# A retention layer and an MLP-mixer block in one kernel: the order of its work planned anew with another model of the transfers

## The chip, the core and the metric

The kernel runs on one core of a Trainium2 chip. The core has a tensor engine (PE, with its weight loads shown apart as PEld), a vector engine (DVE), a scalar engine (ACT), GpSimd (POOL) and a sync engine (SP). Each engine takes its instructions in the order in which the program holds them, and an instruction that has to wait holds up all that stand behind it on its engine. SP, ACT and POOL also issue DMA transfers.

The metric is the device time of one execution, in microseconds (us). Before the change it was 192.45 us in the median of three runs, 190.45 us the lowest and 193.12 us the highest.

## What is computed

```python
# attention part: a decayed running state for each head (4 batches, 8 heads, 768 steps, 64 wide)
for t in range(S):
    state = gamma * state + einsum('bhd,bhe->bhde', k[:, :, t], v[:, :, t])
    y[:, :, t] = scale * einsum('bhd,bhde->bhe', q[:, :, t], state)
x = y with the heads side by side             # 4 x 768 x 512
# mixer part
h = maximum(xT @ w_tok1, 0) @ w_tok2          # over the 768 steps, 256 wide inside
u = x + hT
out = u + maximum(u @ w_ch1, 0) @ w_ch2       # over the 512 channels, 1536 wide inside
```

## The kernel before, in words

**Tiles and stages.** A batch has 768 steps, held as 6 chunks of 128. Its 8 heads are taken in 4 pairs. `front(b, p)` does the attention part and the token mixing for one pair, `back(b)` the channel mixing of a whole batch.

A front works like this. The loads bring k, q and v (lines 464 and 467, issued by POOL). k and q are multiplied by powers of the decay on ACT, DVE or POOL ("decays", lines 506 and 508). k and q are then turned so that channels lie on partitions: for batch 0 and 1 on PE (lines 530 and 532), for batches 2 and 3 by DMA transposes that SP issues (line 520, tiles kT and qT). PE forms the chunk states (561), and DVE runs the decay over them (571, 573). PE forms the scores (599), DVE masks them (609, tile am), and PE sums them with v (621) and with the state (633). Then follow the two products of the token mixing (656 and 676) and the evacuations to x, u and X (line 643). The front ends with turning u into uT, for some pairs on PE (715) and for most by a DMA transpose from SP (705).

A back has a wide part and a narrow part. In batches 0 and 1 the wide part is plain products (749) with a ReLU on ACT (765). In batches 2 and 3 `widen7` forms it from seven products in place of eight (818), for which DVE first takes four differences of uT (line 788, tile hs), ACT keeps partial sums (829) and DVE adds (838). The narrow part is `narrow7` (967 and 977), with sums of h on DVE (931), partial sums kept by ACT (957) and additions to X on DVE (984); its rows go out by DMA (1008), from SP or ACT. The last rows of batch 3 use a plain form (893, 902, 908).

**Modes of PE.** Products with 64 rows or 64 columns (530, 561, 599, 633) run with PE in another shape of its array than the others. The planner's code calls them "high" and "wide" (`tiled`).

**What sets the order.** The kernel first makes a list of 1217 operations (`Op`) with dependencies, buffers and a cost for each engine that may do them. `PRECEDENCE` gives each a rank: it holds two base-36 digits for each operation, in the order of rank. `arrange` then walks through time with a model of five engines, of eight PSUM banks and of the transfers (`Rings`). Whenever an engine is free it takes the operation of lowest rank that the model says is ready. The order in which the operations were taken is the order in which instructions are written, and so the order on each engine; it also decides between ACT and DVE where both can do an operation. The model has no part in the run itself.

`Rings` holds the transfers. The fields of a transfer are a number of steps and the time of one step: `dma=(48, 24)` for a DMA transpose. The queues of SP, POOL and ACT share the transfer engines in rounds, with `MIX` added to a round for each further queue. When the last step is done, the transfer lands `LAND` later, and `PAD` after that once 25 us are past. A transpose that is issued while POOL's queue holds a transfer lands `WAIT` = 4,000 ns later still.

POOL's loads stand in an order written out by hand (`ORDER`), and each must follow the one before it (`behind`). In the first 21 us the program puts PE products of zeros (line 1085) where the plan has PE idle.

Eight of the transfers from SP and ACT can be under way at a time: in the trace they use eight semaphores (101 and 112 to 118) in turn, so the ninth waits for the landing of the first. POOL's loads have eight of their own (103 to 110).

## Time and profile before

| | us |
|---|---|
| median of three runs (lowest, highest) | 192.45 (190.45, 193.12) |
| the profiled execution's own time | 191.84 |
| its span, from the first instruction to the last | 190.1 |
| PE busy | 180.0 (95%), 2347 matmuls |
| DVE busy | 148.3 (78%) |
| ACT busy | 131.2 (69%) |
| POOL busy | 53.0 (28%) |
| PE doing products of zeros (line 1085) | 9.4, 35 matmuls |

The granted clock of PE was 1.00 in all stretches. POOL's queue moved 13.18 MB and its packets took 86.7% of the span of sixteen transfer engines; the queue of SP and ACT moved 10.69 MB and took 35.1%. A DMA transpose of uT landed 7.8 us after its issue in the median (3.0 to 12.0), one of kT or qT 8.5 us (2.7 to 11.0), a load of q 9.4 us (4.6 to 17.0).

A busy PE is not PE at its peak: ends of matmuls are modelled, so that a short stop between two products can be inside "busy". The chain of work that ended last gives the time from one start to the next, and there such stops are seen.

### The profile page before, as it was taken

How to read it: one execution, taken by the hardware profiler on the slowest of the kernel's cores; microseconds unless marked ns; L12 is line 12 of the kernel's file. 1: busy time of each engine (PE TensorE's matmuls, PEld its weight loads, DVE VectorE, ACT ScalarE, POOL GpSimd, SP SyncE). 2: the span in 40 equal slices, each digit the busy share in tenths (PEclk: the TensorE clock that was granted, in tenths of full speed). 3: DMA queues.
4: the chain of work that ended last, by engine and by line, in shares of the span. 5: the costliest groups of instructions: out<-in, count | busy, mean ns of one | idle time of the engine just before them, and what ended most of it. 6: DMA issues, size and time to landing. Idle time of an engine off the chain costs nothing.

```text
span 190.1 us, 5757 instructions
## 1 busy us (share of the span) xinstructions
PE 180.0 (95%) x2347; PEld 134.5 (71%) x2347; DVE 148.3 (78%) x401; ACT 131.2 (69%) x306; POOL 53.0 (28%) x62
## 2 busy tenths in 40 slices
PE   7987797999999999999999999799999999999993
PEld 3544686666678889667778889556578996656882
DVE  4698885823999996945199799498999959997982
ACT  6367599599689956689987956679864363665120
POOL 8995676550395013055002820000000000000000
PEclk9999999999999999999999999999999999999999
DMA  6999999999999999999999999992200168000116
GB/s 106 170 156 195 184 177 182 182 205 203 167 157 155 111 157 186 118 198 191 134 134 136 157 171 150 202 237 45 43 3 0 59 124 240 2 0 0 59 57 221
DMA packets 94236, 25.54 MB, mean 134 GB/s; under 512 B 84353, under 2 KB 91265, under 8 KB 94209
## 3 DMA queue, kind: packets, MB, share of 16 engines
q0 software_dynamic: 67456, 13.18, 86.7%
q1 hardware_dynamic: 26032, 10.69, 35.1%
q10 hardware_dynamic: 720, 1.31, 2.4%
q8 instruction: 18, 0.29, 0.7%
q14 instruction: 10, 0.07, 0.1%
HBM read 26.74 MB, written 6.29 MB: 174 GB/s over the span
## 4 chain that ended last, share of the span: by engine, by line
PE 78%; DMA 10%; POOL 4%; DVE 3%; issue 1%; ACT 1%; DVEq 0%; POOLq 0%; ACTq 0%
PE bank L749 17%; PE bank L818 13%; PE bank L967 13%; PE bank L977 10%; DMA uT<-u 6%; PE bank L676 6%; PE bank L656 5%; DMA v<-in_v_dram 5%; PE bank L893 3%; PE bank L599 3%; PE bank L621 2%; PE bank L561 2%; POOL k L467 2%; PE bank L633 2%; PE bank L530 1%
## 5 line engine op out<-in xcount | busy, mean ns | idle before, releaser
L609 DVE TENSOR_TENSOR am<-bank,mask 128x384 f16<-128x384 f32 x64 | 31.6, 547 | 8.0 <-PE bank L599 7.7
L749 PE MATMUL bank<-uT,wc 128*128 128x384 f16 x192 | 36.2, 327 | 0.0
L467 POOL DMA_DIRECT2D v<-in_v_dram x16 | 16.5, 1032 | 48.7 <-PE bank L621 43.8
L765 ACT ACTIVATE h<-bank 128x384 f16<-128x384 f32 x48 | 22.8, 513 | 4.7 <-PE bank L749 4.3
L749 PEld LDWEIGHTS <-wc 128*128 128x128 f16 x192 | 16.9, 98 | 9.8 <-DVE U L573 0.5
L829 ACT COPY us<-bank 128x384 f32<-128x384 f32 x36 | 16.7, 490 | 8.6 <-PE bank L818 5.4
L957 ACT COPY us<-bank 128x256 f32<-128x256 f32 x33 | 12.2, 380 | 15.0 <-PE bank L967 13.0
L984 DVE TENSOR_TENSOR X<-X,bank 128x256 f32<-128x256 f32 x44 | 17.8, 413 | 4.2 <-PE bank L977 3.7
L838 DVE TENSOR_TENSOR h<-bank,us 128x384 f16<-128x384 f32 x36 | 18.7, 550 | 2.6 <-ACT us L829 1.6
L967 PEld LDWEIGHTS <-hs 128*128 128x128 f16 x198 | 18.5, 98 | 2.5
L573 DVE SCALAR_TENSOR_TENSOR U<-U,gp,bank 128x64 f32<-128x64 f32 x64 | 17.0, 277 | 1.3
L643 ACT CAST u<-bank 128x384 f16<-128x384 f32 x31 | 14.9, 496 | 4.2 <-PE bank L676 4.1
L967 PE MATMUL bank<-wsum,hs 128*128 128x256 f16 x132 | 17.7, 273 | 0.0
L643 ACT CAST x<-bank 128x384 f16<-128x384 f32 x31 | 14.0, 484 | 5.1 <-PE bank L621 3.8
L467 POOL DMA_DIRECT2D k<-in_k_dram x15 | 15.5, 1034 | 3.3 <-DVE U L573 1.1
L506 ACT ACTIVATE k<-k,gk 128x384 f16<-128x384 f16 x21 | 12.7, 619 | 4.6 <-DMA k<-in_k_dram 3.6
L643 ACT COPY X<-bank 128x384 f32<-128x384 f32 x32 | 15.6, 503 | 0.0
L676 PE MATMUL bank<-h,wt 128*128 128x64 f16 x384 | 15.3, 193 | 0.0
L676 PEld LDWEIGHTS <-wt 128*128 128x128 f16 x384 | 14.1, 98 | 1.6
L818 PE MATMUL bank<-hs,late 128*128 128x384 f16 x72 | 14.5, 326 | 0.3 <-ACT us L829 0.2
L931 DVE TENSOR_TENSOR hs<-h 128x768 f16<-128x768 f16 x18 | 9.8, 550 | 5.3 <-ACT h L765 5.3
L977 PEld LDWEIGHTS <-h 128*128 128x128 f16 x132 | 12.5, 98 | 1.9
(84 smaller groups left out, 342.7 us busy)
## 6 DMA issues: line engine op xcount, KB each, us to landing
...
q<-in_q_dram POOLq DMA_DIRECT2D x16, 192.0 KB, 9.4
v<-in_v_dram POOLq DMA_DIRECT2D x16, 192.0 KB, 9.2
k<-in_k_dram POOLq DMA_DIRECT2D x15, 192.0 KB, 10.6
...
```

Source lines behind the costliest of these rows:

```text
L467: (nc.sync if hard else nc.gpsimd).dma_start(out=tile_of(s, [P, 2, NC, D], FP if hard else F16), in_=src.rearrange("h (c p) d -> p (h c) d ...
L573: nc.vector.scalar_tensor_tensor(out=u[:, c], in0=u[:, c - 1], scalar=gp[:, p:p + 1], in1=st, op0=ALU.mult, op1=ALU.add)
L609: nc.vector.tensor_tensor(am, SC[g].tile[:, :m * P].rearrange("p (i t) -> p i t", t=P), mask.to_broadcast([P, m, P]), ALU.mult)
L643: (nc.scalar.copy if e == "ACT" else nc.vector.tensor_copy)(tile(), cols(src.tile[:, :S // 2]))
L676: nc.tensor.matmul(Y[j].tile[:, i * D:(i + 1) * D], wt2[:, jt, t], H1.tile[:, jt, j * D:(j + 1) * D], start=False, stop=(jt == NJ - 1), sk ...
L749: nc.tensor.matmul(acc[:, :SH], wc1[:, ct, ft * P:(ft + 1) * P], UT.tile[:, ct, sh * SH:(sh + 1) * SH], start=(ct == 0), stop=(ct == NP - 1))
L765: nc.scalar.activation(H2.tile[:, ft], A.tile[:, :SH], AF.Relu)
L818: nc.tensor.matmul(acc[:, :SH], left(ct), r[:, ct], start=first and ct == 0, stop=ct == C2 - 1, skip_group_check=True)
L838: nc.vector.tensor_tensor(h(m, sh), R.tile[:, :SH], KS.tile[:, j], ALU.add)
L967: nc.tensor.matmul(acc_[:, lo], l[:, j], r[:, j], start=first and j == 0, stop=j == K2 - 1, skip_group_check=True)
L977: nc.tensor.matmul(acc_[:, lo], l[:, j], r[:, j], start=first and j == 0, stop=j == K2 - 1, skip_group_check=True)
L984: (nc.vector if e == "DVE" else nc.gpsimd).tensor_tensor(dst(), dst(), b_(), ALU.add)
```

## The change

The model of the transfers is altered, a rule for the eight semaphores comes in, and `PRECEDENCE` is another list of the same 1217 operations. `MIX` and `SLOW` (which was 1.0) go. In place of `MIX`, POOL's queue takes `PULL` = 2.2 shares of a round whenever another queue is active. `WAIT` now holds for all transfers from SP and ACT after 25 us, stores too, and not for transposes from SP alone. A transpose has steps of 16.6 ns in the model and not 24. `lane` has a transfer from SP or ACT wait, in the model, for the landing of the eighth before it. `arrange` makes the new order from the new ranks by this model. No operation, tile, buffer, hand-written order or cost of PE, ACT or DVE is altered, and neither is what an operation emits. [...]

```diff
--- before.py
+++ after.py
@@ -44,9 +44,8 @@
     FIRST = dict(SP=600, POOL=1300, ACT=700)
     LAND = dict(SP=900, POOL=1900, ACT=2000)
     DT = 40.0
-    MIX = 8.0
+    PULL = 2.2
     WAIT = 4000
-    SLOW = 1.0
     PAD = 300
 
     def __init__(self):
@@ -59,7 +58,7 @@
         end = first + op.dma[0] * self.GEN[q]
         self.made[q].append(end)
 
-        late = self.WAIT if q == "SP" and op.dma[0] == 48 and self.line["POOL"] else 0
+        late = self.WAIT if q != "POOL" and start > 25000 and self.line["POOL"] else 0
         self.line[q].append([op, float(op.dma[0]), first, end, late])
 
     def busy(self):
@@ -69,11 +68,10 @@
         dt, t = self.DT, self.t
         on = [(q, l[0]) for q, l in self.line.items() if l and l[0][2] <= t]
         if on:
-            round_ = sum(x[0].dma[1] for _, x in on) + self.MIX * (len(on) - 1)
-            if t > 25000:
-                round_ *= self.SLOW
+            share = {q: self.PULL if q == "POOL" and len(on) > 1 else 1.0 for q, _ in on}
+            round_ = sum(share[q] * x[0].dma[1] for q, x in on)
             for q, x in on:
-                n = dt / round_
+                n = share[q] * dt / round_
                 if x[3] > t:
                     n = min(n, dt / self.GEN[q])
                 x[1] -= n
@@ -101,7 +99,7 @@
     free = dict(FREE)
     taken = {t: [] for t in BUFS}
     bank_slot = {i: None for i in range(8)}
-    sp_made = [0, 0, 0]
+    lanes = []
     waiting = {e: [] for e in ENGINES}
     for o in ops:
         for w in o.ways:
@@ -172,6 +170,12 @@
                     m = max(m, x)
         return m, banks
 
+    def lane(o, e):
+        if o.dma is None or e == "POOL" or len(lanes) < 8:
+            return 0
+        x = end[lanes[-8].n]
+        return INF if x is None else x + SEM
+
     left = n
     while left:
         moved = False
@@ -190,6 +194,7 @@
                         wake = min(wake, r)
                     continue
                 m, banks = room(o)
+                m = max(m, lane(o, e))
                 if m > t:
                     if m < INF:
                         wake = min(wake, m)
@@ -211,6 +216,8 @@
                 free[e] = at + way[1]
                 if o.dma:
                     rings.add(e, o, t)
+                    if e != "POOL":
+                        lanes.append(o)
                     if e == "SP":
                         free[e] = max(t + way[1], rings.made["SP"][-3])
                 else:
@@ -256,29 +263,29 @@
 
 
 PRECEDENCE = (
-    "0c312g322j2i0b0k380a07342535420h432n0i27300j28000403080105020e0d2209230g0f2444332h2k3e3d260l3y293i2l2m3z3f2a"
...
-    "c6c7atbeavkhktkibfauc8ljbga31mbhawc9bil4caa4cba7bja61nl5cca8a5cd9mjk999nai9c9o9d9pjnlvaacel6a9laajlkaxlbcfkj"
...
-    "b6cid3m5mncjn5d5dvd4chm6d6modwd7n6bqd8dxclmp1ocnd9e1dabtmqdbe2mse4mre5e6cmdydzbumte31pcomue0lme7ln1qbvmacpmb"
-    "mxlobw1rmcbzcqbxmzmyc01smvn0byncc2n1crn3c1mw1tcvnlcsn2n4dcctnmn8cwddcunrcycxnon9nansegnnnpnbdfdenqdgnendntdh"
-    "n7nunfngdinvdje8njdknhe9dleanyecfndmebnznwnifonkdno3euevfpnxdoo7o0dpo4ewo9eddqefereseeo1obo6o8osetocodo2ouog"
...
-    "orp7p4fup3p8p9fvopekpqelpsfxp6prpefyq7emptpvpfpgpufzphpwpbpienpcpyeopopjpzpxeqpdepplpppkq0q5f4qof8pmq6q2q1f5"
...
+    "0a070900050b04010c0302080d060e340f35420g43220h262327240i2530310j322f0k332g2h282j3d290l3g3e3y3i3z2a3f400m4w4x"
...
+    "a2kld1atlba3bdlcl8bea4bfl9kybga5bhkzbikma6knl0aubja71mkobkava8bmldaw1nleaabla9kvaxbokwlfbpbnbrd2aykxbqd3d51o"
+    "dvdwc9d4d6l1d7azl2cabsd8lgcbl3d9b0dxccbtdalhcdb1kscektdbm7b2m8cfb3dydzlmbukue0b4lnmdlimjmfbvb5b6ljmem9bzmklo"
...
+    "e6dhcse7mldi1tm5ctlvculwm6mmlxdje8mnfnfocvecdkmqfpebcwmae9eumbeamrnpcydlmumcmvernlmxedesdmmwnmnqmyeefqnrnnet"
+    "cxnoefevnunsdno7ewfrn5ntego8donvn6fsehexo9ftdpdreydqfueiezdsfvf0fwnydtduf1fxejf2nwfynzoaf3f4nxfzo3f8f5eko0f7"
+    "elf6enemmzn3eoo1f9epn0eqfan4fbg0n1fcn8o4fdg1o6nag4n9g2fenbncn2ffg3nendn7fgo2nhfhnfo5fjfingobfkodninjocosfmoz"
...
 )
@@ -519,7 +526,7 @@
                     t = tile_of(dst, [P, S], F16)
                     nc.sync.dma_start_transpose(out=t.rearrange("d (c t) -> d c t", t=P),
                                                 in_=src.tile.rearrange("p c h d -> p (c h d)"))
-                return Op(ops, (PLACE[b, p], 0, b, p, 0), [("SP", 1200, 1200, emit)], dep, [dst], [src], dma=(48, 24))
+                return Op(ops, (PLACE[b, p], 0, b, p, 0), [("SP", 1200, 1200, emit)], dep, [dst], [src], dma=(48, 16.6))
             T = Slot(FA)
 
             def emit():
@@ -705,7 +712,7 @@
                 nc.sync.dma_start_transpose(out=UT.tile[:, p].rearrange("d (c t) -> d c t", t=P),
                                             in_=U16.tile.rearrange(flat))
             e = Op(ops, (PLACE[b, p], 0, b, p, 99), [("SP", 1200, 1200, emit)], casts + [None if opens else first_of[b, "uT"]],
-                   [UT] if opens else [], [U16] if opens else [U16, UT], dma=(48, 24))
+                   [UT] if opens else [], [U16] if opens else [U16, UT], dma=(48, 16.6))
         else:
             T = Slot(FA)
 
```

More of the change, by code (lines that the diff above doesn't have):

```diff
@@ L258 @@
 PRECEDENCE = (
-    "0c312g322j2i0b0k380a07342535420h432n0i27300j28000403080105020e0d2209230g0f2444332h2k3e3d260l3y293i2l2m3z3f2a"
-    "400m4w4x3g414y2b3h0n2e4z362c3j2d3k37390o3a4b3b2o3c2f4e2p3l453m4d3n0p462q4748492r4a0q504c514g0r4f2s595b2t4h5c"
-    "4i0s2w2v3o524j3p532u0t2x544k3q552y565a4l0u3t2z5d3r4m3s575e585f0v5u5y5v3u5h5g4n5z3w3v4o0w5i6u3x5j4r4p6v5k0x4q"
-    "4s6q5w0z6r4u4t5x5m0y4v5p06675ngs6a5o6s5q69gj5r6b5s6t686w605t6xgm116y616c6zgt62hm7063hn7164gn72hs65ht66gk6dgl"
-    "127q6egu7rh76fgoh8hj136ghkhdh9hehl7n6h7m14hogp6igqhf7sgr7o7thu6j7u7pi77v157wgv7xh46kh17yh26lhph3hqi8hr10ha16"
@@ L264 @@
-    "i95lhb6mhc736nh5746o6phyh676gwhz7517gx7z77gy8178hv8279gz80hg83h0hhhwi0181uhi84i1hxi21w8520i37a8o867bjb1v87ig"
-    "7c19ijih8iia1xiiib7d8j1ajc88ili4icik7e1bi58pim8mi68q7i8n1c8k9f7f9g89jx8r1y8l1didie8s7ginif1eiu7h8t1zio8b8uis"
-    "1f7jjr9iip217l8a7k8eitjt8civ9jiwjs8d9kiqiy8f1gjuixjv8gjyizae8hj1irjwafj08v9hagj2j3j98wj48zk0ab8xack28yk1ad90"
-    "jz92jalsj5k4k3lg91ldj6lek6k51hjej8k7k9jfjdk895kakb96kc1ib7jib8jgjjb9jp9397jh9a989l9bak9e9qjl9sal9rjoj79v94jq"
-    "9u9wlhlfamltjmanm1m29tlikdlukem3kmkfl1l29zah9xl3ao9yaskvc31jkwaqkga0l7arl8l9kx1kbdksapc4a1knc5babb1lkoa2kubc"
@@ L269 @@
-    "c6c7atbeavkhktkibfauc8ljbga31mbhawc9bil4caa4cba7bja61nl5cca8a5cd9mjk999nai9c9o9d9pjnlvaacel6a9laajlkaxlbcfkj"
-    "llkkaylcczd0kykzklckkpd1azkql0lykrb3bklzb0mdm0mhb1mfb2memimgb4m7bmbsb5lwm8bnlxlpm9lqmjblbolrm4mkbpbrmlcgd2mm"
-    "b6cid3m5mncjn5d5dvd4chm6d6modwd7n6bqd8dxclmp1ocnd9e1dabtmqdbe2mse4mre5e6cmdydzbumte31pcomue0lme7ln1qbvmacpmb"
-    "mxlobw1rmcbzcqbxmzmyc01smvn0byncc2n1crn3c1mw1tcvnlcsn2n4dcctnmn8cwddcunrcycxnon9nansegnnnpnbdfdenqdgnendntdh"
-    "n7nunfngdinvdje8njdknhe9dleanyecfndmebnznwnifonkdno3euevfpnxdoo7o0dpo4ewo9eddqefereseeo1obo6o8osetocodo2ouog"
@@ L274 @@
-    "oaeho5drqbqmfcqzqhr0qnrvq4fdr1otoeexohofoxovdsozoyeyojduowdtezf0fqp0okf1frolp1oqfsfwpap5f2ejomonoip2f3eiftoo"
-    "orp7p4fup3p8p9fvopekpqelpsfxp6prpefyq7emptpvpfpgpufzphpwpbpienpcpyeopopjpzpxeqpdepplpppkq0q5f4qof8pmq6q2q1f5"
-    "qqqppnf6q3qrqtf7q8qvf9quqcqefaqdqwqsgdqxqfshq9rrqas0r3rwqgrsfeqyr4rtqjsjffqiskr2sds2s1qkrusifgses4qlfhslsmsg"
-    "fis5s3fbg7g0sfsns6g3g4s9g2sog1rxs7sag5s8g6spr9sbg8ryg9r5t4fjsqrzfkr6tkscragaflr7fmsrrer8gbtnrgrfgcrhgfrbggss"
-    "gercgighrdristrksurjsxrlrmrnsvrpt3rosyu1szrqtdt0uit5t1tlt8t2tpt9tmt6tat7tbtstouptttrtitutztjtftetvu0twtgvnvi"
@@ L279 @@
-    "txujswu3thu2tyunu4u6u8tquouku5u7uzuluqu9urx5uauxugubusumuyuuutuhuducuvvgv1uev0x6uwvhufxqxlv2v4vlvjv5v3vmvkxm"
-    "v6v7vov8w1tcvpv9vevqvvvfvbvavrvwvsvcwnvtx7wjx8vuwowkx9xawlwsvdxbwuwmwtxcw3vxwvw2wpvzvywyw4w6w0wqw8w7w5wrwww9"
-    "wzwawxwcx0wbxnx3wdwewgwhxexdx1wiwfxfx4xhx2xixgxoxjxkxrxsxp"
+    "0a070900050b04010c0302080d060e340f35420g43220h262327240i2530310j322f0k332g2h282j3d290l3g3e3y3i3z2a3f400m4w4x"
+    "412b4y2i3h0n4z363j2c3k372d2l382e2k0o392n3a4b3b2m4d443c4e2o3l0p452p4c46473m4g3n0q48504f492q514a2r0r5a2s5e2v5d"
@@ new lines @@
+    "2t4h3o0s2u2w523p4i2x534j0t59544k3t555b2y4l563q0u5c2z4m573r585f5g4n0v5u5y3u5v5h3s5z4o3v3w5i0w4r4p3x5w5j6u5x4s"
+    "5k0x6q4q6r4t6v4u5l6s4v0y5m676tgj685n0z5p6a5ogs695q606b5r105s616c625t6w636d6411gp6x656ygk66gq6zhp70glhq71gr7q"
+    "726e7rhj6fgt12hd6gheguhkhf6h13hlhghrhh6i73147m7nh774hi6j75h86k777sh9gm766lgn7thm157ugohn7vh17who7x7o7yh2h47p"
+    "h56mh37816h67a7z6n79816ogy6pgz7b80gv7c82gwh0ha83gx177dhb7ehvhcighwijidhxieil18ih1uifipiiinik1v84i4io19i58iim"
+    "7i8j7f1xi6hs1aht7g1wi17hi21bhu85iq7j8oir8ki37l8p867k8q1c8m8r8l9fiu8n9ghy1dhz87iv9his1y88i0ia1eit8s8920iw8a8t"
@@ new lines @@
+    "1ziy8uix1f8b9i9j8e218cjb9k8dizib8fjci7icj01gi88h8g8vaeafj18zj3ag8xj9abj2i9jv8wacj48yjxadjrb790j592b891js9ljw"
+    "1hb9ahj693k0ja9mj8941ijejtk195j7jfjuk496jdjyjik59njzk2c39oai9pjj97ajc4k3k9ak989qc5aljg99amka9r9ajhank6kc9bjk"
+    "babbk79c9dk8bc9s9ejljn9vkb9tl4c6kp9uc7kd9wkekqc8jmkf9xl5jokr9ykgl6jq1j9zjpaoa0khara11kkjaqkikkl7czap1llad0as"
+    "a2kld1atlba3bdlcl8bea4bfl9kybga5bhkzbikma6knl0aubja71mkobkava8bmldaw1nleaabla9kvaxbokwlfbpbnbrd2aykxbqd3d51o"
+    "dvdwc9d4d6l1d7azl2cabsd8lgcbl3d9b0dxccbtdalhcdb1kscektdbm7b2m8cfb3dydzlmbukue0b4lnmdlimjmfbvb5b6ljmem9bzmklo"
@@ new lines @@
+    "momgbwmpcgbxmscibyc0cklklpc1chc2m1llmtm2cjlym3lzclcmm0cndc1pcolqdgcplsdd1qlrltdfe1lucqde1re2mhe3cre41sm4e5mi"
+    "e6dhcse7mldi1tm5ctlvculwm6mmlxdje8mnfnfocvecdkmqfpebcwmae9eumbeamrnpcydlmumcmvernlmxedesdmmwnmnqmyeefqnrnnet"
+    "cxnoefevnunsdno7ewfrn5ntego8donvn6fsehexo9ftdpdreydqfueiezdsfvf0fwnydtduf1fxejf2nwfynzoaf3f4nxfzo3f8f5eko0f7"
+    "elf6enemmzn3eoo1f9epn0eqfan4fbg0n1fcn8o4fdg1o6nag4n9g2fenbncn2ffg3nendn7fgo2nhfhnfo5fjfingobfkodninjocosfmoz"
+    "floeogotoiofnkp9ohoxouoyojovg5p0okowg6p1g7olpqg8p2p7g9onomp3p8oqoop4orpgopprp5pxgap6papvgbpepwpbpfpspcpygcpt"
@@ new lines @@
+    "pzphpdgdq7puq0pigfgeq5q1pjq2ggqoq6pkgiq3plghqvq4q8qqpmpopnqpqcq9ppqrqtqdqeqaquqfqsqbqwqgrvqxqhqmqyr3qnqiqjqz"
+    "r4r0qkr9rrshr1rwsjrsrts0r2qls2sds1rusirxs3ses4rys6sfs5rzsms7sgs9sns8rbr5sbsqsarar6soscsrr7rercsprgskrfr8ssrh"
+    "rirdstrkslrjsusvrlsxrnrmszrpt3rotkt4t0uirqtlt5t1t8t2tpt9tmt6tqtaswtbt7tssytntctrtottuptdtituvntjtftetvtwtgu1"
+    "uktxujvgthtzu2tyulunu0u6umuov1u3u7uqu4u9uruzu5uau8usuxubuguyuuutucuhuduvx5uev6vhviuwv0ufxlvlvjv4v2vmx6v5vkxm"
+    "v3vov7vpw1v8vqvvv9vevwvsvrvavfvbvtwnwjx7vuwowlx8wkx9xavcwuvdxbwswvxcwmw3wtvxwyw4w2vzwpvyw8w5w0w6w9wwwqw7wzwc"
@@ L282 @@
+    "wrwxwax0wdx1x3wbxnwewfx2whxdxowgx4xexpwixqxfxgxrxhxixsxjxk"
 )
```

## The prediction

> **What bounds the kernel now.** The first page says that PE is the engine to look at:

> ```profile
> span 190.1 us, 5757 instructions
> ...
> PE 180.0 (95%) x2347; PEld 134.5 (71%) x2347; DVE 148.3 (78%) x401; ACT 131.2 (69%) x306; POOL 53.0 (28%) x62
> ```

> An order can't make products shorter; it can only take time out in which PE does none. So I looked for that time next, by the busy time in six stretches (columns: stretch, its length, then busy time of PE, PEld, DVE, ACT, POOL):

> ```profile
> 0.00:20.00 20.00, 16.50 (x211) 9.72 (x211) 14.40 (x61) 11.60 (x20) 15.76 (x24) 1.00 1.59 158
> 20.00:34.00 14.00, 12.19 (x288) 10.53 (x287) 10.61 (x25) 11.40 (x27) 10.26 (x12) 1.00 1.83 182
> 34.00:120.00 86.00, 85.89 (x1205) 66.30 (x1203) 65.00 (x164) 69.93 (x166) 27.02 (x27) 1.00 1.81 161
> 120.00:126.00 6.00, 4.72 (x67) 3.04 (x64) 3.85 (x11) 3.84 (x10) 0.00 (x0) 1.00 1.19 253
> 126.00:186.00 60.00, 59.88 (x582) 44.45 (x581) 53.57 (x144) 34.42 (x85) 0.00 (x0) 1.00 0.24 60
> 186.00:190.10 4.10, 0.79 (x8) 0.47 (x5) 0.84 (x2) 0.00 (x0) 0.00 (x0) 1.00 0.56 203
> ```

> PE stands still for 3.5 us before 20, 1.8 us up to 34, and 3.3 us after its last product (one addition and the last store). Between 34 and 186 it is filled, but for one hole at 120 to 126. The chain of work that ended last names its cause, and one more stop:

> ```profile
> 31.69 1.07 issue
> ...
> 74.84 0.43 PE bank L561 x20
> 75.28 0.76 PE bank L977 x6
> ...
> 76.38 0.66 PE bank L967 x6
> ...
> 110.35 0.86 ACT u L643 x2
> 111.24 11.15 DMA uT<-u
> 122.48 0.56 DVE hs L788
> ```

> The transpose of the last uT of batch 2, issued at 111.24, took 11.15 us, and `widen7` of batch 2 waited for it. PE's timeline there shows what that cost:

> ```profile
> 121.28 0.98 PE L818 MATMUL bank<-uT,wc 128*128 128x384 f16 x5
> 122.43 0.32 PE L818 MATMUL bank<-uT,wc 128*128 128x384 f16 x1 [0.18 <-DMA uT<-u]
> 123.65 0.48 PE L818 MATMUL bank<-uT,wc 128*128 128x384 f16 x2 [0.90 <-DVE X L984]
> 123.98 0.51 PE L676 MATMUL bank<-h,wt 128*128 128x64 f16 x12
> 124.32 0.49 PE L818 MATMUL bank<-hs,late 128*128 128x384 f16 x2
> 124.74 0.35 PE L561 MATMUL bank<-v,k 128*64 128x64 f16 x10
> ```

> The next product starts at 125.29, so these took 4.0 us. Their work is ten L818 at 0.163 us, twelve L676 at 0.029 us (0.70 us for 24 in the chain) and one group of L561 (0.28 us): 2.26 us. 1.75 us are lost, 0.2 us of it changes of mode; **the hole is worth 1.6 us**. "DVE X L984" is the same wait at second hand: the addition stood on DVE behind a difference (L788) that had waited 2.2 us for uT.

> **The change, part by part.** No operation is added or taken away, so the sum has only waits and changes of mode. I read both lists, two digits at a time, and added up the PE time that the code gives the PE operations between two places. One us of it is 1.033 us on the clock: the first transpose of uT stands at 28.8 in the old list and was issued at 47.53, the last of batch 2 at 90.5 and at 111.24. That a place in a list is a place in the program is true only nearly, since the model decides at each step; distances can be off by some tenths.

> 1. *The hole.* From the transpose `cy` to the first product that needs it, `ob`, the old list has 8.2 us of PE work (8.5 on the clock), and the landing took 11.15: too late by 2.7. The new list has 15.4 us (15.9). Even the longest landing of a uT, 12.0 us, ends before. The 1.6 us go. If it doesn't work, they stay; a gain above 1.6 isn't there. What is late next is below, under 3 and 4.

> 2. *Changes of mode.* In the chain six products of L977 take 0.76 us right behind L561, and six products of the narrow part 0.66 us elsewhere: a change costs 0.10 to 0.11 us, and PE's busy time hides it. Leaving out the first 20 us of PE work, where PE waits anyway, the old list changes mode 54 times, the new one 46. Eight times 0.11 us: −0.9 us, with −0.3 to −1.2 as its ends, since `arrange` may part a group again.

> 3. *Fronts of batches 2 and 3 come earlier, the narrow part of batch 1 later.* This puts new waits where engines stand in order. Three places have less room than before:
>    - The second difference on DVE, `o8`, stands 3.8 us (3.9) behind `cy`; it was 8.5. What stands behind it on DVE are masks, states and the additions that free PE's banks. By the new list the last load, `1t`, goes out 4.4 us (4.5) ahead of `cy`. In the trace the transposes at 118.94 and 120.37, with the last two loads still landing until 122.17, landed after 5.36 and 5.31 us; the one at 123.42, with none, after 4.43. I take 5.4, so DVE waits 1.5 us. PE has six banks for this batch, and six products of 0.65 us are 3.9 us of cover. So PE loses little: 0.3 us. The ends: nothing, or 11.15 − 3.9 − 3.9 = 3.4 us if it lands as late as before.
>    - The scores of the third pair of batch 3, `f4`, stand 3.9 us (4.0) behind their transpose `ew`; it was 13.2. PE itself waits here, without cover. With no load under way landings were 2.75 to 4.43 us, with two 5.3: between 0 and 1.4 us, and I take 0.4.
>    - The decays of q of the second pair of batch 3, `dy`, stand 6.0 us (6.2) behind their load `1n`; it was 16.3. In the trace this load, issued at 88.83, landed after 13.7 us, and loads that were alone landed after 5.2 (102.93) and 6.5 us (83.15). The decays run on ACT or DVE, and behind them on ACT stand the ReLUs (L765) that free the banks. Between the ends, 0 and 13.7 − 6.2 = 7.5 us of wait, I take 10 us for the landing, since the old flight had five transposes in it and the new list has three: a wait of 3.8 us, which six banks (3.9 us) nearly hide. 0.5 us.

> 4. *The rule for eight semaphores, and stores that land later.* They are in the model only. In the trace no transfer of SP or ACT was held by its semaphore at the issues around the hole: the one at 111.24 reused a semaphore free since 102.34. Nothing, ±0.3 us.

> 5. *Start and end.* POOL's hand-written order stays, and with it the landings that PE waits for up to 20 us; the last operations of both lists are of the same kinds. Nothing, but DVE's order within the first 20 us is another, and PE waited 0.6 to 1.1 us at single places there: ±1.0 us.

> 6. *Blocks of instructions.* At 31.69 the chain has 1.07 us of "issue": PE stops between two products of one group (L599) without any wait. PE's instruction queue fetched 18 packets of 16 KB in the run, one of them from 30.41 to 31.33. The stop can stay, go or come twice: 0, with ±1.1 us. [...]

> The sum for the profiled execution: 191.84 (its span of 190.1 and 1.7 us around it) − 1.6 − 0.9 + 0.3 + 0.4 + 0.5 = 190.5 us. The median of the runs shown lies 0.6 us above the profiled one, so a median after is **191.1 us**, 0.7% less. No change and 2% of one are about what a measurement of this kernel can just tell apart, so this counts as no change.

> **The rivals.**

> *A wait for loads takes the place of the wait for uT, and it is slower.* Place: the decay `dy`. Price: if its load needs 13.7 us as before, ACT stands for 7.5 us; the banks cover 3.9, PE loses 3.6 in place of 0.5: 194.2 us as a median. If the banks are held already when the wait begins, all 7.5 are lost: 198.1 us. It decides from a landing of about 10 us. For it: in the old flight of this load POOL's queue was just as full. Against it: fewer transposes share the flight, and no ACT wait for a load is in the trace after the start.

> *The order only moves the hole.* Everything in 3 takes as much as 1 and 2 give: 192.4 us. For it: three in-order waits with less room, where the old list had one.

> *More comes than I count.* The waits in 3 are all covered (−1.2), the stop at 31.69 goes (−1.1) and the start gains 0.6: 188.2 us. For it: the model's new figures shorten loads and lengthen transposes, and in the trace the transposes were what came late. Against it: three independent gains.

> **How the numbers follow.** Forecast (189.5 to 192.0): 0.45. Hole moved (192.0 to 193.5): 0.20. Slower by loads: 0.25, two thirds of it above 196.3, where 2% slower lies, since cover is scarce when ACT and DVE are behind. More than counted: 0.10, nearly all below 188.6, where 2% faster lies. So faster by over 2%: 0.10; slower by over 2%: 0.17; within: 0.73. The range goes from 187.8, a little under the case of more, to 196.3 us; it leaves out 0.17 above, the case without cover, and about 0.03 below.

> **What the next profile would show.** Right: between 105 and 130 no uT in the chain with ten or more us; PE's stretch there filled; 46 to 50 changes of mode after the start; DVE's wait before L788 at 1.5 us or less. Wrong: ACT idle before L506 waiting for k or q between 75 and 100 with PE's busy time below 9.5 of 10 us there; PE idle before L599 for qT or kT. The forecast falls if a landing beside loads still takes 11 us with the new order, or if the first 34 us lose more than 1 us.

## The result and the profile after

| | before | after |
|---|---|---|
| median of 4 runs each (lowest, highest), us | 191.45 (190.14, 193.12) | 200.8 (199.72, 201.7) |
| the profiled execution's own time and span, us | 191.84, 190.1 | 201.07, 199.3 |

After takes 1.051 times as long as before (95% interval 1.040 to 1.062). The forecast was 191.1 us with a range up to 196.3, and the kernel is slower than every case that I had priced, the case without cover (198.1 us) among them. Below, ratios leave out executions more than 1.5% above the fastest of their kernel, and for e2 and e6, which came out at two times with one and the same program, all four times are given and no ratio.

The first page of the changed kernel, its lines on the span and the engines:

```profile
span 199.3 us, 5756 instructions
...
PE 182.8 (92%) x2348; PEld 136.0 (68%) x2348; DVE 148.3 (74%) x401; ACT 132.2 (66%) x306; POOL 52.8 (27%) x62
```

The span is 9.2 us longer, and PE is busy for 2.8 us more with the same products (one more of zeros). So PE both stands still for longer and runs slower somewhere. The busy time by stretches of the changed kernel says where (columns: stretch, its length, busy time of PE, PEld, DVE, ACT, POOL, then PE's granted clock, DMA share, GB/s):

```profile
0.00:20.00 20.00, 15.97 (x206) 9.11 (x206) 14.37 (x62) 12.05 (x21) 15.59 (x23) 1.00 1.59 160
20.00:34.00 14.00, 11.53 (x276) 10.21 (x276) 9.72 (x23) 11.30 (x26) 10.28 (x12) 1.00 1.81 182
34.00:78.00 44.00, 44.00 (x623) 33.94 (x619) 36.27 (x89) 36.91 (x86) 15.87 (x16) 1.00 2.02 160
78.00:106.00 28.00, 22.16 (x278) 14.92 (x276) 12.15 (x34) 18.01 (x43) 6.05 (x6) 0.88 1.68 167
106.00:128.00 22.00, 21.57 (x344) 17.12 (x343) 16.03 (x43) 17.94 (x45) 5.05 (x5) 1.00 1.08 123
128.00:195.00 67.00, 66.56 (x626) 50.01 (x624) 58.92 (x152) 36.03 (x88) 0.00 (x0) 1.00 0.23 67
```

The same view of the kernel before, for the stretch that differs most:

```profile
78.00:106.00 28.00, 27.89 (x380) 20.00 (x379) 18.11 (x51) 24.52 (x60) 6.85 (x7) 1.00 1.73 161
```

From 78 to 106 us PE did 278 products where it had done 380, and the clock was 0.88. The hole at 120 to 126 is gone: PE is busy for 21.57 of the 22 us from 106 to 128.

A finer measure is used for the rest. For each product I took the time to the start of the next one, and took off what the same product takes undisturbed (0.163 us for L749 of before, 0.109 for L967 and so on). What remains is PE's loss: waits, changes of mode, and the slower clock. Summed by stretches, in us:

| | 0–21 | 21–34 | 34–78 | 78–106 | 106–end | sum |
|---|---|---|---|---|---|---|
| before | 14.8 | 2.9 | 3.0 | 2.2 | 4.4 | 27.2 |
| after | 14.5 | 4.2 | 3.0 | **10.8** | 4.0 | 36.4 |

Of the 9.2 us, 8.6 are in one stretch. PE's timeline of the changed kernel shows the stops in it (in brackets the idle time ahead of a group, and what ended it):

```profile
81.16 0.32 PE L640 MATMUL bank<-r,qT 64*128 64x64 f16 x10
83.38 0.82 PE L606 MATMUL bank<-qT,kT 64*128 64x128 f16 x12 [1.90 <-DMA kT<-k]
...
89.39 0.35 PE L568 MATMUL bank<-v,k 128*64 128x64 f16 x10 [1.02 <-ACT h L772]
...
96.00 0.51 PE L568 MATMUL bank<-v,k 128*64 128x64 f16 x20
98.69 0.81 PE L756 MATMUL bank<-uT,wc 128*128 128x384 f16 x4 [2.18 <-ACT h L772]
```

The first stop is a wait of the scores for the transposed k of batch 2's second pair, issued at 73.13 and landed at 83.33, 10.2 us later. The other two, one short and one long, are waits for a ReLU that frees a bank. The waits of the engines from 78 to 106 us say what held the ReLUs (us in total, times, longest):

```profile
DVE k L515 <- DMA k<-in_k_dram: 3.7, 1, 3.7
...
ACT q L513 <- issue: 2.7, 1, 2.7
ACT k L513 <- DMA k<-in_k_dram: 2.4, 1, 2.4
PE bank L756 <- ACT h L772: 2.2, 1, 2.2
...
DVE q L515 <- DMA q<-in_q_dram: 2.0, 1, 2.0
PE bank L606 <- DMA kT<-k: 1.9, 1, 1.9
```

ACT stood in front of the decays of k and q of batch 3's first pair, and DVE in front of k of its second pair. (The 2.7 us of ACT before its q are that too: the profile names no releaser, but ACT went on at 97.65, just behind the landing of q at 97.57.) Their loads took 17.0 us (issued 70.73, landed 87.77), 15.4 (82.20, 97.57) and 15.4 us (83.20, 98.62). Behind them on ACT stand the ReLUs, as the first rival of the prediction has it.

The flights themselves are not new. In the kernel before, the transfers issued from 64 to 78 us took as long (count, size, median us from issue to landing), and PE lost 2.2 us from 78 to 106:

```profile
k<-in_k_dram POOLq DMA_DIRECT2D x1, 192.0 KB, 16.7
...
kT<-k SPq DMA_TRANSPOSE x2, 10.4
```

This load is k of batch 3's first pair, which took 17.0 us in the changed kernel. What is new is when its user comes. The first stop was close in the kernel before, too: its transpose landed at 81.99, and the scores began at 82.07.

The clock is the other part. Windows of 2 us of the changed kernel; the third column from the right is the granted clock:

```profile
82.00:84.00 2.00, 0.62 (x12) 0.56 (x12) 0.00 (x0) 0.21 (x1) 2.00 (x3) 0.84 1.28 148
84.00:86.00 2.00, 2.00 (x10) 0.89 (x7) 1.77 (x4) 1.14 (x3) 0.23 (x1) 0.50 1.29 114
86.00:88.00 2.00, 2.00 (x24) 1.49 (x23) 0.18 (x1) 0.15 (x1) 0.00 (x0) 0.81 1.21 160
...
100.00:102.00 2.00, 2.00 (x18) 1.27 (x18) 0.98 (x5) 1.99 (x6) 0.00 (x0) 0.60 2.32 152
102.00:104.00 2.00, 2.00 (x10) 0.96 (x9) 0.32 (x1) 1.77 (x4) 0.00 (x0) 0.54 1.97 140
```

After each of the two long stops PE ran at half its clock for 3.41 us (83.35 to 86.77 and 100.42 to 103.83), and so lost 1.7 us more each time. Together that is 3.4 us of the 9.2, and it looks like work: PE is "busy" there with ten products in 2 us.

### The profile page after: what moved, and what is told of

Same layout as the page of the kernel before. It is cut to its first block, busy times and chain, and to the rows that moved or that the text cites. A ratio compares the mean times of both kernels' runs of the same rounds, so it can differ in the third digit from the quotient of the medians.

```text
span 199.3 us, 5756 instructions
## 1 busy us (share of the span) xinstructions
PE 182.8 (92%) x2348; PEld 136.0 (68%) x2348; DVE 148.3 (74%) x401; ACT 132.2 (66%) x306; POOL 52.8 (27%) x62
## 4 chain that ended last, share of the span: by engine, by line
PE 49%; issue 24%; DMA 14%; POOL 10%; DVE 1%; POOLq 0%; ACT 0%
PE bank L825 14%; DMA q<-in_q_dram 10%; PE bank L974 9%; PE bank L984 7%; PE bank L756 5%; POOL v L474 4%; PE bank L683 3%; DMA k<-in_k_dram 3%; PE bank L900 3%; POOL k L474 3%; PE bank L663 2%; POOL q L474 2%; PE bank L628 1%; DMA qT<-q 1%; PE bank L606 1%
## 5 line engine op out<-in xcount | busy, mean ns | idle before, releaser
L616 DVE TENSOR_TENSOR am<-bank,mask 128x384 f16<-128x384 f32 x64 | 32.1, 550 | 14.5 <-PE bank L606 14.5
L756 PE MATMUL bank<-uT,wc 128*128 128x384 f16 x192 | 39.8, 344 | 3.1 <-ACT h L772 2.2
L474 POOL DMA_DIRECT2D v<-in_v_dram x16 | 16.3, 1025 | 55.9 <-PE bank L628 23.1
L756 PEld LDWEIGHTS <-wc 128*128 128x128 f16 x192 | 17.9, 102 | 14.0 <-issue 6.4
L964 ACT COPY us<-bank 128x256 f32<-128x256 f32 x33 | 12.1, 374 | 18.0 <-PE bank L974 16.0
L836 ACT COPY us<-bank 128x384 f32<-128x384 f32 x36 | 16.3, 483 | 7.3 <-PE bank L825 5.4
L650 ACT CAST u<-bank 128x384 f16<-128x384 f32 x32 | 15.8, 493 | 6.4 <-PE bank L683 4.7
L580 DVE SCALAR_TENSOR_TENSOR U<-U,gp,bank 128x64 f32<-128x64 f32 x64 | 16.3, 276 | 1.0
L650 ACT CAST x<-bank 128x384 f16<-128x384 f32 x32 | 14.5, 494 | 3.1 <-DMA kT<-k 2.1
L474 POOL DMA_DIRECT2D k<-in_k_dram x15 | 15.4, 1031 | 3.3 <-DVE U L580 1.2
L683 PE MATMUL bank<-h,wt 128*128 128x64 f16 x384 | 16.2, 194 | 0.0
L683 PEld LDWEIGHTS <-wt 128*128 128x128 f16 x384 | 14.7, 99 | 2.0 <-issue 0.2
L825 PE MATMUL bank<-hs,late 128*128 128x384 f16 x72 | 15.2, 326 | 0.0
L663 PE MATMUL bank<-x,wt 128*128 128x128 f16 x192 | 13.5, 219 | 0.7 <-issue 0.7
L513 ACT ACTIVATE k<-k,gk 128x384 f16<-128x384 f16 x19 | 11.1, 618 | 4.2 <-DMA k<-in_k_dram 4.2
L984 PEld LDWEIGHTS <-h 128*128 128x128 f16 x132 | 12.6, 98 | 1.8
## 6 DMA issues: line engine op xcount, KB each, us to landing
q<-in_q_dram POOLq DMA_DIRECT2D x16, 192.0 KB, 9.6
v<-in_v_dram POOLq DMA_DIRECT2D x16, 192.0 KB, 9.6
k<-in_k_dram POOLq DMA_DIRECT2D x15, 192.0 KB, 10.6
wc<-in_moe_w_ch_dram POOLq DMA_DIRECT2D x2, 256.0 KB, 10.3
```

Source lines behind the costliest of these rows:

```text
L474: (nc.sync if hard else nc.gpsimd).dma_start(out=tile_of(s, [P, 2, NC, D], FP if hard else F16), in_=src.rearrange("h (c p) d -> p (h c) d ...
L616: nc.vector.tensor_tensor(am, SC[g].tile[:, :m * P].rearrange("p (i t) -> p i t", t=P), mask.to_broadcast([P, m, P]), ALU.mult)
L650: (nc.scalar.copy if e == "ACT" else nc.vector.tensor_copy)(tile(), cols(src.tile[:, :S // 2]))
L663: nc.tensor.matmul(acc[:, jt * P:(jt + 1) * P], wt1[:, i, jt * P:(jt + 1) * P], X16.tile[:, i].rearrange("p h d -> p (h d)"), start=(i == ...
L683: nc.tensor.matmul(Y[j].tile[:, i * D:(i + 1) * D], wt2[:, jt, t], H1.tile[:, jt, j * D:(j + 1) * D], start=False, stop=(jt == NJ - 1), sk ...
L756: nc.tensor.matmul(acc[:, :SH], wc1[:, ct, ft * P:(ft + 1) * P], UT.tile[:, ct, sh * SH:(sh + 1) * SH], start=(ct == 0), stop=(ct == NP - 1))
```

## The experiments

"Room" is the PE time that stands in the planned order between a load and the decays that need it. The losses are by the measure above.

### Is it the list or the model?

**e1** gives the changed model the list of before.

```diff
--- after
-PRECEDENCE = (the new list)
+PRECEDENCE = (the list of before)
```

> The changed kernel with the old list of ranks: only the model of the transfers is new. If the list is what costs (theory), the order is nearly that of before, the hole at 120 to 126 stays, and the time is 191 to 194 us. If the model alone already makes a bad order (rival), for instance by other choices between ACT and DVE, it is 197 us or more.

Measured: 203.03 us, ratio 1.056 (1.047 to 1.064). The rival held: the model alone costs as much as the whole change. In e1's order PE's operations stand 0.4 places off those of before in the mean, at most 12; but the decays of batch 3 stand nearer to their loads (room for q of the first pair 5.0 us in place of 14.6, k of it 7.5 in place of 18.6, k of the second pair 9.0 in place of 15.2), and the transposes of batch 2's last pairs stand earlier. PE lost 13.3 us from 78 to 106. Its longest stop, in the timeline of the profiled execution of e1 (204.33 us):

```profile
91.04 1.61 PE L606 MATMUL bank<-qT,kT 64*128 64x128 f16 x12 [6.82 <-ACT h L772]
```

**e4** keeps the order of the start and takes the rest from the new list.

```diff
--- after
-PRECEDENCE = (the new list)
+PRECEDENCE = (the first 270 ranks of the old list, then the others in the order of the new)
```

> The changed kernel with a mixed list: the first 270 ranks in the old order, the others in the new order. Theory (the loss sits between 75 and 105 us, where the new list puts the transposes and decays of batches 2 and 3 earlier): the stops there stay, 198 to 201 us; the 1.4 us lost in the first 45 us may come back. Rival (the lag from the start, some 1.5 us, is what pushes the later places out of step): the stops go, and the time is below 195 us.

Measured: 199.83 us, ratio 1.044 (1.039 to 1.049), with 9.4 us lost from 78 to 106. The start has no visible part in the loss.

**e7** has the old model with the list of e4.

```diff
--- before
-PRECEDENCE = (the list of before)
+PRECEDENCE = (the list of e4)
```

> The model of the kernel before; the first 270 ranks of the old list, the rest in the order of the new. In the order that results the loads of batch 3 have 13 to 17 us of room, as before, and uT of b2's last pair 9.3 us in place of 7.7. Theory (the model's room, not the list, costs the time): 189 to 192, the kernel before or 1 us better, no hole at 120, clock at 1.0. Rival (the new list costs it, as in e4 with 199.8): 197 or more.

Measured: 199.02 us, ratio 1.038 (1.029 to 1.047). The sum speaks for the rival, the profiled execution doesn't: its clock stays at 1.0 and the stretch from 78 to 106 loses 3.4 us, with no stop over 0.6 us. The time is lost elsewhere, at the start of batch 3's wide part, in a hole that this order has by itself (PE's timeline of e7):

```profile
161.52 1.30 PE L818 MATMUL bank<-uT,wc 128*128 128x384 f16 x7
165.73 0.32 PE L818 MATMUL bank<-uT,wc 128*128 128x384 f16 x1 [2.91 <-DMA uT<-u]
```

So e7 doesn't tell whether the list costs by itself. It only suggests, as e1 shows, that the loss at 78 to 106 comes with the model, and that for the profiled execution: in two of the others the mean clock, 0.982 and 0.989, tells of one or two stretches at half clock whose place was not traced.

### What meets at 70 to 100 us?

**e3** leaves seven loads out: v of batch 2's last pair and k, q and v of batch 3's first two pairs, which POOL fills with a constant.

```diff
--- after
+if b == 3 and p < 2 or (b, p, what) == (2, 3, "v"):
+    nc.gpsimd.memset(t_, 0.125)
+else:
     (nc.sync if hard else nc.gpsimd).dma_start(out=t_, in_=...)
```

> The changed kernel without seven loads: v of the last pair of batch 2 and k, q and v of the first two pairs of batch 3 are filled with a constant by POOL, so their data are left out. Order and everything else as in the changed kernel. Theory (loads and transposes collide between 60 and 100 us): transposes after 70 land after 3 to 6 us in place of 10 to 12, SP holds each for about 1.3 us in place of 2 to 4, ACT and DVE don't wait for k and q, PE has no stop of 1 us between 75 and 105, the clock stays at 1.0, and the time is 190 to 192.5 us. Rival (SP is behind by its own work, whatever POOL loads): the first stop, for the transposed k at 81.4, stays, and the time is 196 us or more.

Measured: 190.97 us, ratio 0.999 (0.996 to 1.002). The stretch from 78 to 106 loses 1.9 us, and what comes after 106 loses 2.2 where before lost 4.4:

```profile
78.00:106.00 28.00, 28.00 (x423) 20.65 (x420) 18.75 (x52) 24.23 (x58) 7.69 (x10) 1.00 0.91 135
```

With those loads gone the transposes issued from 72 to 92 us land in 3 to 6 us.

**e12** leaves the other side out, the six stores of batch 0 (batch 0 of the output is not written).

```diff
--- after
-(nc.sync if e == "SP" else nc.scalar).dma_start(out=out[b, i * P:(i + 1) * P, :], in_=X.tile[:, i])
+if b > 0:
+    (nc.sync if e == "SP" else nc.scalar).dma_start(out=out[b, i * P:(i + 1) * P, :], in_=X.tile[:, i])
```

> The changed kernel without the six stores of batch 0 (1.5 MB, issued at 65 to 88; batch 0 of the output is left out). Theory (loads and transposes collide, and the stores are a lesser part of it): the transposes at 70 to 85 land 2 to 3 us sooner, the stop at 81 goes with the fall of the clock, the waits for loads at 88 and 96 shrink: 194 to 197. Rival A (without the stores there is no collision at all, as without the loads in e3): 190 to 193. Rival B (stores have no part in it): 199 or more.

Measured: 192.12 us, ratio 1.006 (1.003 to 1.010). By its time that is rival A, against my expectation: 1.5 MB of stores are as needed for the loss as the loads are. By its mechanism it isn't, since the transfers still meet. The clock stays at 1.0 in the profiled execution, the transposes of k at 71.91 to 75.27 still take 8.7 to 10.3 us, but they are issued 1 to 2 us sooner, since no store stands ahead of them on SP, and the loads at 82 and 83 land after 8.4 and 9.6 us in place of 15.4. The first stop is gone by little: the transpose landed at 81.48, and the scores began at 81.53. Two stops stay, for decays that wait for loads (e12's timeline):

```profile
93.74 0.48 PE L756 MATMUL bank<-uT,wc 128*128 128x384 f16 x2 [1.22 <-ACT h L672]
98.94 0.82 PE L984 MATMUL bank<-wc,h 128*128 128x256 f16 x6 [1.08 <-ACT h L772]
```

**e2** fills the stop at 81 us: ten products of zeros ahead of the scores of batch 2's second pair.

```diff
--- after
+if (b, p) == (2, 1):
+    for _ in range(10):
+        nc.tensor.matmul(SC[run[0]].tile[:, :384], zero[:, :P], zero, start=True, stop=True)
```

> The changed kernel with ten products of zeros (10 x 0.163 us) ahead of the scores of the second pair of batch 2, in the bank that these scores take. In the changed kernel PE waits there from 81.4 to 83.4 us for a transpose, and the granted clock is 0.5 from 83.35 for 3.41 us. Theory: the clock falls because PE stood still; with 1.6 us of the wait filled it stays at 1.0 there, and the run gains 3.41 x 0.5 = 1.7 us, to about 199 us; the later fall at 100.4 stays or moves. Rival: the clock falls for another reason; then it falls all the same and the time stays at 200.8 us or grows.

Measured: 194.29, 200.16, 201.67 and 202.26 us. The profile is of the first: the clock stays at 1.0, and the transposes at 70 to 82 us land after 5 to 7 us where the changed kernel's took 10 to 12. The zeros are not why: they ran at 83.3 us, and in this execution the loads issued from 50 to 63 us had already landed after 6.5 to 9.8 us, in place of 9.5 to 16.4. Its start was other: at 48 us it was 1.9 us behind the changed kernel. So the run tells nothing on the zeros, and nothing on the price of the clock; e8 and e9 do that.

### The room of the loads, and the meeting of loads and transposes

**e5** makes the changed model believe that loads issued after 60 us land 7 us later, so that their decays stand farther behind them.

```diff
--- after
+        if q == "POOL" and start > 60000:
+            late = 7000
         self.line[q].append([op, float(op.dma[0]), first, end, late])
```

> The changed kernel, but its model lets every load issued after 60 us of plan time land 7 us later. The list and all else stay. In the order that results, the decays of k and q stand farther behind their loads: q of b3's first pair 12.4 us of PE work in place of 7.4, k of the second pair 13.1 in place of 7.5, q of the second pair 12.6 in place of 6.0. Theory (the new order leaves the loads of batch 3 too little room, and DVE and ACT stand in front of them): the stops of PE at 88 (1.35 us) and 96.3 (2.38 us) go, and with them the second fall of the clock (1.7 us): 5.4 us off 200.8, so 195.4; 194 to 197. Rival (the transfers collide whatever the room, and the wait only moves to the transposes behind the decays): 199 or more.

Measured: 197.92 us, ratio 1.035 (1.027 to 1.042), between the two theories. The stops at 88 and 96 and the second fall of the clock are gone, as the theory has it (6.1 us lost from 78 to 106), but the order after 106 is another too and loses 5.4 us in place of 4.0.

**e6** does the same to e1 (5 us, after 40 us).

```diff
--- e1
+        if q == "POOL" and start > 40000:
+            late = 5000
         self.line[q].append([op, float(op.dma[0]), first, end, late])
```

> The kernel of e1 (the old list in the changed model, 203.0 us), but its model lets every load issued after 40 us land 5 us later. The decays of batch 3's first pairs get 10 to 12 us of room in place of 5 to 9; the transposes of batch 2's last pairs are issued 2 us later than in e1, and still 6 to 8 us sooner than in the kernel before. Theory (room of the loads): most of the 11 us that e1 lost come back, 192 to 196. Rival (what costs is that the transposes are issued sooner, into the loads): 200 or more.

Measured: 193.29, 194.41, 200.36 and 203.29 us: both theories, in one kernel. In the profile of the first the transposes at 72 to 83 us land after 5.1 to 8.5 us. So this profile, like that of e2, shows quick transfers, and not what the room does when they are slow. The room alone doesn't secure the shorter time.

**e10** adds to e5 that two loads start only when a transpose has landed: POOL reads one column of kT of batch 2's second pair before it issues v of batch 2's last pair, and k of batch 3's first pair stands behind it.

```diff
--- e5
+            if (b, p, what) == (2, 3, 'v'):
+                nc.gpsimd.tensor_copy(zero[:, :1], turned[2, 1][:, :1])
             if wide:
                 nc.gpsimd.dma_start(...)
```

> The kernel of e5 (197.9 us), and POOL reads one column of kT of batch 2's second pair before it issues the load of v of b2's last pair, so that this load and that of k of b3's first pair start only when the transpose has landed. Nothing else moves in the program. Theory (these two loads, under way from 70 to 87, are what keeps the transposes in flight for 10 to 12 us): the transposes issued at 72 to 78 land after 4 to 7 us, the stop at 81 (2.59 us) and the fall of the clock behind it (1.7 us) go: 193.6; 192 to 195.5. Rival (the transposes and stores hinder each other without loads, or the loads are then missed at 88 to 95): 197 or more.

Measured: 194.17 us, ratio 1.016 (1.010 to 1.021), as the theory said. The transfers issued from 72 to 78 us, of the changed kernel and then of e10:

```profile
out_dram<-X SPq DMA_DIRECT2D x1, 256.0 KB, 8.3
...
kT<-k SPq DMA_TRANSPOSE x3, 11.2
```

```profile
out_dram<-X SPq DMA_DIRECT2D x1, 256.0 KB, 5.5
kT<-k SPq DMA_TRANSPOSE x3, 4.8
```

The same three transposes land in less than half the time. The two loads, issued 10 us later, land at 86.25 and 88.41; in the changed kernel they landed at 81.88 and 87.77. The second landed 0.6 us later for starting 10 us later.

e5 and e10 moved PE's order as well. **e13, e14 and e15** part the two causes with PE's order of the changed kernel kept, or nearly so (in e13 and e14 operations stand 0.2 places off in the mean, at most 7): room alone (loads of 60 to 86 us land 6 us later in the model), the reading of kT alone, and both.

```diff
--- after, e13 and e14
+        if q == "POOL" and 60000 < start < 86000:
+            late = 6000
--- after, e13 and e15
+            if (b, p, what) == (2, 3, 'v'):
+                nc.gpsimd.tensor_copy(zero[:, :1], turned[2, 1][:, :1])
```

> The changed kernel with both remedies and, on PE, nearly its own order (operations stand 0.1 places off in the mean): loads issued from 60 to 86 us of plan time land 6 us later in the model (decays of batch 3's first two pairs 11 to 17 us of PE work behind their loads, in place of 6 to 12), and POOL reads a column of kT of batch 2's second pair before it issues the two loads of 70 us. Theory (these two causes make the whole loss): in the changed kernel PE lost 10.8 us from 78 to 106 us, with both remedies 2.2 as in e10; 200.8 - 8.6 = 192.2, 191 to 193.5, clock 1.0. Rival (something else of the new order costs as well): 195 or more.

> As e13 without POOL's reading of kT: the room alone. Theory: the stop at 81 and one fall of the clock stay (3.8 us), the waits for loads at 88 to 99 go with the second fall: PE loses 6.1 us from 78 to 106 as in e5; 200.8 - 4.7 = 196.1, 195 to 198. Rival (with PE's order kept, the room alone doesn't help, and e5's gain came from its other order): 199 or more.

> The changed kernel with POOL's reading of kT alone: the decays keep their little room. Theory (both causes count): the stop at 81 goes with its fall of the clock (3.8 us), k of b3's first pair is missed by 2 us instead of 1.4, and the loads behind it land 3 to 6 us sooner than in the changed kernel, so that the stop at 96 shrinks below what makes the clock fall (3 us or more): 200.8 - 3.8 + 0.7 - 3 = 194.7; 193.5 to 196.5. Rival (the room decides: the loads, started 9 us later, are missed by 5 us and more): 198 or more.

| | time, us | ratio (interval) | lost 78–106 | lost 106–end |
|---|---|---|---|---|
| after | 200.8 | 1.051 (1.040–1.062) | 10.8 | 4.0 |
| e14, room | 198.57 | 1.035 (1.026–1.043) | 7.8 | 4.6 |
| e15, reading kT | 199.23 | 1.039 (1.031–1.047) | 9.7 | 3.1 |
| e13, both | 195.54 | 1.019 (1.013–1.026) | 2.8 | 5.5 |

The last two columns are of the profiled executions. Alone each takes little of the loss from 78 to 106 away, 3.0 and 1.1 us; together they take 8.0 of the 8.6 us. e14 keeps the slow transposes (2.26 and 2.13 us of wait for kT and qT). e15 has quick transposes, but its loads start 10 us later while the decays keep their place, and one decay stops everything (waits and PE's timeline of e15):

```profile
ACT k L516 <- DMA k<-in_k_dram: 6.8, 1, 6.8
```

```profile
85.20 0.49 PE L761 MATMUL bank<-uT,wc 128*128 128x384 f16 x2
92.14 0.48 PE L573 MATMUL bank<-v,k 128*64 128x64 f16 x10 [6.45 <-ACT h L777]
```

I had expected that wait to be 2 us: 88.4, the landing in e10, less the time at which the changed kernel wanted k, already delayed by the stop at 81. With that stop gone the decay is reached sooner, and the load landed at 90.52. In e13 the stretch is repaired:

```profile
78.00:106.00 28.00, 27.92 (x419) 19.98 (x417) 18.57 (x47) 24.54 (x58) 10.08 (x11) 1.00 1.68 180
```

But e13 is 195.5 and not 192.2 us. Against my sum, the first 21 us lose 1.0 more (a stretch of half clock at 8 us), 78 to 106 loses 0.6 more, and what comes after 106 loses 1.5 more, in small stops at 110, 122 and 127 us (0.5 to 0.7 us of idle time each). Those are figures of the profiled execution (195.49 us). Four of the six, 194.88 to 195.62 us, had a mean clock of 0.998 to 1.0 and so no stretch at half clock, and were hardly quicker for it; what keeps the median up is not fully found. None of the kernels beats before.

### The clock by itself

**e8** puts three stops into the kernel before, after the crowd of transfers: PE waits until POOL has cleared a tile six times. (Two loads still land up to 124.8 us beside the first stop, at 122.75.) **e9** has two clearings in place of six.

```diff
--- before
+if b == 2 and j4 and i in (1, 3, 5):
+    nc.tensor.matmul(acc[:, :SH], zero[:, :P], zero, start=True, stop=True)
+    for _ in range(6):          # e9: range(2)
+        nc.gpsimd.memset(zero, 0.0)
+    nc.tensor.matmul(acc[:, :SH], zero[:, :P], zero, start=True, stop=True)
```

> The kernel before, with three stops of PE put into batch 2's widen7, where no load is under way any more: PE waits each time until POOL has cleared a tile of zeros six times (about 6 x 0.39 us, with two products of zeros beside it of 0.16 us and two signals). Theory (a stop of some 2.5 us makes the clock fall to one half for 3.41 us, which costs 1.7 us more): 3 x (2.5 + 0.33 + 1.7) = 13.6 us, so 205 us, and three stretches at 0.5. Rival (the stop costs only itself, and the falls in the changed kernel have another cause): 3 x 2.8 = 8.5 us, 200 us, clock at 1.0.

> As e8, with two clearings in place of six, so each stop is shorter by 4 x 0.39 = 1.6 us: in e8 the three stops were 3.24 to 3.30 us from the product of zeros to the next, so here 1.7. Theory (a stop of about 2 us is needed to make the clock fall): the clock stays at 1.0 and the kernel loses the three stops alone, 3 x (1.7 + 0.2) = 5.6 us, 196.7 us. Rival (any such stop makes it fall): three more stretches at 0.5 of 3.41 us, 5.1 us more, 201.8 us.

Measured: e8 203.37 us, ratio 1.062 (1.054 to 1.070); e9 195.7 us, ratio 1.022 (1.015 to 1.029). The profile of e8 is of its longest execution, 207.5 us: each stop was 3.24 to 3.30 us from product to product, and behind each the clock fell, behind the first for twice 3.41 us. In e9 they were 1.34 to 1.40 us, and it never fell. Around the second stop of e8, then of e9:

```profile
135.40:138.80 3.40, 0.57 (x14) 0.32 (x11) 1.88 (x7) 0.91 (x3) 2.42 (x6) 1.00 0.08 15
138.80:142.20 3.40, 3.25 (x11) 1.58 (x12) 0.82 (x2) 1.66 (x4) 0.09 (x1) 0.51 0.00 0
```

```profile
132.00:135.40 3.40, 2.33 (x17) 1.29 (x14) 2.35 (x8) 1.94 (x6) 0.83 (x2) 1.00 0.08 16
135.40:138.80 3.40, 3.00 (x29) 1.72 (x26) 2.49 (x8) 3.23 (x8) 0.28 (x1) 1.00 0.14 27
```

At the second stop of e8 15 GB/s were moved, against 148 and 156 at the long stops of the changed kernel, so behind this stop the clock fell without a crowd of transfers. But not behind each stop: the other executions of e8 took 202.53, 202.72 and 204.02 us at mean clocks of 0.991, 0.992 and 0.983, which is room for one, one and two stretches of 3.41 us at half clock behind three stops (an estimate: what the mean clock lacks to 1.0, times the span, over 1.7 us). e9's 4.2 us are about its three stops of 1.4 us and nothing else.

### The gain at 120 us by itself

**e11** is the kernel before, with the transpose of the last uT of batch 2 landing later in the model.

```diff
--- before
+        if late and 104000 < start < 1000000000:
+            late = 7000
         self.line[q].append([op, float(op.dma[0]), first, end, late])
```

> The kernel before with its list and its model, but a transpose issued after 104 us while POOL's queue holds a load lands 7 us later in the model, in place of 4. It is the gain of the changed kernel at 120 taken alone: in the plan other products stand where the hole is. Theory (the hole is worth 1.6 us, and the rest of the order stays as good): 189.3 to 190.5. Rival (the products that fill it are missed elsewhere): 191 to 192, as before.

Measured: 191.93 us, ratio 1.002 (0.998 to 1.006): the rival. From 106 to the end it loses 3.7 us in place of 4.4. The hole shrinks to one stop at 124.1, 0.76 us from the start of one product to the next, and the rest of its 1.6 us isn't in the median.

## Why the prediction was wrong

**Step 1, the hole** was right. The last uT of batch 2 was issued at 120.84 and landed after 2.82 us, and no wait for it is left. (With so short a landing the room of before, 8.5 us, would have done as well; so the larger room is not put to the test here.) **Step 2**: changes of mode after 33 us went from 60 to 53; in undisturbed products one costs 0.11 us, so 0.8 us for the forecast 0.9. Both gains are seen only in e3 and e12, which leave transfers out: there the time after 106 loses 2.2 and 2.1 us where before lost 4.4, which is the 2.5 us of the forecast but 0.3. In e13, which repairs the stretch with all transfers in place, it loses 5.5, so the gain is not shown for a whole kernel. In the changed kernel 0.4 of it is left: a late load gives a new small stop at 119 (0.68 us from product to product) and a late transpose one at 128 (0.72).

**Step 3 failed**, at the words "Three places have less room than before". I had looked for the least room in the new list and priced the one at `dy` (q of batch 3's second pair, 16.3 to 6.0 us). The same reading of the lists gives eight loads of batch 3 with less: q of the first pair 15.9 to 7.4 us, k of the second 16.8 to 7.5, k of the first 17.3 to 12.3, and k and q of the last two pairs 11 to 15 against 5 to 6 (`dy` is the eighth). `dy` itself came out near the forecast: its load landed after 9.7 us (10 forecast) and DVE waited for 2.0. The loads ahead of it, with 15.4 and 17.0 us of flight, made the stops. The other two: `o8` cost nothing, and the scores `f4` made the stop of 0.72 us at 128 (0.4 forecast).

The first stop is no loss of room in the plan. The code of both kernels plans the transpose of k of batch 2's second pair as far ahead of its scores (13.5 us of plan time before, 13.3 after). On the chip SP issued it at 71.47 before and at 73.13 after: the issue ahead of it took 3.45 us in place of 1.73, and a store of batch 0 that ACT issued before now stands ahead of it on SP. With the 0.08 us that the kernel before had to spare, that made the stop. Such a place, and the time that SP takes for its issues, no step had.

The first rival, a wait for loads before the decays with the ReLUs behind them on ACT, was right in kind, and so was its point of decision, a landing of more than 10 us. The sign named for it came: ACT stood idle for k and q, and PE was busy for 7.1 of 10 us from 80 to 90 and again from 90 to 100. I gave it 0.25 and set its place one pair too late. What spoke against it was the count of transposes in the flight, and a load "alone" at 83.15 that wasn't alone: the next two loads were issued 1.0 and 2.0 us behind it, and k of 71.67 was under way until 88.41. That count was the wrong quantity: e10 and e12 show that it matters whether loads, stores and transposes are under way at the same time (the three transposes landed after 4.8 us in e10 and 11.2 us in the changed kernel, the loads of 82 and 83 us after 8.4 and 9.6 us in e12 and 15.4 us in the changed kernel), and in e10 the load of k landed only 0.6 us later for starting 10 us later.

**Step 4** asked only whether the rule for eight semaphores does anything; planned again without it, the order is the same operation by operation. The other figures of the model, `PULL` and the 16.6 ns, I used as an argument for the hopeful rival: "the model's new figures shorten loads". That is what did the harm. A shorter load in the model puts its decay nearer in the program, and the chip's loads got no shorter. Flights of three loads of batch 3, in us, as `arrange` of each kernel has them and as the traces have them:

| | plan before | chip before | plan after | chip after |
|---|---|---|---|---|
| k, first pair | 18.3 | 16.7 | 12.0 | 17.0 |
| q, first pair | 15.1 | 9.3 | 7.5 | 15.4 |
| k, second pair | 15.3 | 12.0 | 7.8 | 15.4 |

The old figures were long enough for all three, the new ones for none, and e1 shows the loss with the old list. Which of the new figures does most of it was not tried.

**No step had the clock.** The prediction read a clock of 1.00 in all stretches and took a wait to cost its own length. Two waits of 1.9 and 2.2 us cost 1.7 us more each, 3.4 of the 9.2 us: nearly double what such a term of the sum would have had.

**Step 5** held for the first 21 us (14.8 against 14.5 lost). **Step 6**: the chain of the changed kernel has two stops of "issue" inside a group early on, the second right behind a wait for a mask on DVE, where before had one of 1.07 us:

```profile
26.37 0.74 issue
...
33.10 0.75 issue
```

From 21 to 34 us it loses 1.3 us more, a little beyond the ±1.1 of that step. What makes these two stops no run here shows. In the trace a 16 KB packet of the instruction queue (q8) had ended ahead of each, at 25.61 and 32.24 us, as one had at 31.33 ahead of the stop of before; but behind the packets that ended at 38.73 and 45.52 us the chain has no such stop.

What stays open: why the same program can find its transfers quick or slow, in e2 from 50 us on (e2, e6). A reading that fits is that slow transposes hold SP (issues of 1.5 to 4.0 us in the changed kernel at 65 to 77 us against 1.2 us undisturbed), which keeps them beside the next loads and stores. The kernel before has issues as long (1.7 to 3.8 us at 65 to 76 us), and the reading was not tested apart from e10 and e12.
